# Loading and centring w_out ahead of chunk 1, and one table of 1/sqrt for chunk 0, in an attention-then-SoLU kernel

## The chip, the cores and the metric

The kernel runs on one core of one Trainium2 chip. The metric is the time of one execution in device microseconds (us). A profile is of one execution and its span is 1.7 to 1.8 us shorter than the timed run, so differences inside a profile are compared with differences inside another, and times with times.

## The reference, cut to what matters

```python
# q, k, v: (8, 8, 576, 64) float32
kv  = einsum('bhsd,bhse->bhde', k, v)                 # one 64x64 matrix per head
o   = einsum('bhsd,bhde->bhse', q, kv)
x   = o / sqrt(mean(o*o, -1) + 1e-6) * g_norm         # (4608, 512) after a transposition
h   = x @ w_in                                        # 512 -> 1024
solu = h * softmax(h)
out = layernorm(solu) * g_ln @ w_out                  # 1024 -> 512
```

The kernel folds the layer norm into the last product: `w_out` is scaled by `g_ln` and its column means are taken off ("centred") once, and each row of `out` is multiplied at the end by one number (`rstd`) that comes from three sums over `h` ("sums").

## The kernel before: what the change and the argument touch

The work is cut into nine chunks of 512 tokens. Every piece of work on an engine, and every load, is put into a plan with an engine, an estimated length and a rank. A small scheduler runs through the plan once, while the program is built, and the order that it finds is the fixed order of the instructions on each engine. On the chip only the engines' own order and the semaphores count: an engine that waits holds up everything behind it, and a transfer starts when its issuing engine comes to it.

```python
class Plan:
    def order(self):
        free, done, queue, lanes, mode = {}, {}, 0.0, [], {}
        ...
            done[n] = t + length + {"pe": 0.2, "sp": 2.5}.get(engine, 0.12)
            if load:                       # the model of a load: one queue, 'load' us each
                queue = max(queue, t + length + 1.0) + load
                done[n] = queue + 1.0
                lanes.append(done[n])
```

The loads are issued by POOL (GpSimd), which also does squares (`usq`) and sums of exponentials (`es`) between them. q of the chunks 0 to 3 is turned by TensorE; from chunk 4 on a transposing transfer, issued by SP, does it from SBUF to SBUF.

```python
    XBAR = tuple(range(4, NC))
    ...
    for b in range(B):
        behind = [] if b < 2 else [("x", (0, 1, 1))] if b == 2 else [("h_mm", b - 3, 2)]
        ...                                # k and v of chunk b: pool, load=3.0 each; q: pool, load=2.7
    plan.add("w_out", "pool", 0.9, -1.2, load_w_out, load=5.4)
    ...
    def q_turn(c):
        t = T["qT", c] = tile_of(("qT", c), [128, H, 2, 128], BF16)
        nc.sync.dma_start_transpose(
            t.rearrange("q h y p -> q (h y) p"), T["q", c].rearrange("p h j d -> p (h j d)")
        )
    ...
        if c in XBAR:
            plan.add(("qT", c), "sp", 4.0, r - 0.1, lambda c=c: q_turn(c), ...)
    ...
    def s_ln(*i):                          # 1/sqrt as exp(-0.5 ln): two passes on ACT
        nc.scalar.activation(out=t[:, :], in_=T["s", i][:, :], func=AF.Ln, bias=eps_t[:, :])
    def s_exp(*i):
        nc.scalar.activation(..., in_=T["lss", i][:, :], func=AF.Exp, scale=-0.5, bias=zero_t[:, :])
```

`h_mm` is h of a chunk (eight groups of four products), `out` the last product, `o_mm` the product of q with kv, and `usq` and `es` what POOL and ACT prepare for the sums.

The softmax here doesn't subtract the row's maximum and nothing guards it: scores larger than these inputs give would overflow.

## Time and profile before

| | before |
|---|---|
| time, median of 4 runs (range) | 202.06 us (200.93 to 203.91) |
| span of the profile, mean granted clock | 200.5 us, 1.00 |
| TensorE busy | 184.0 us, 92% of the span |
| third product of h (h goes on) | 22.29 us |
| sums of chunks 0, 1, 2, 3 begin | 47.01, 67.77, 85.89, 103.93 us |
| sums of the last chunk begin | 189.35 us |

The sums of each chunk are the landmarks of this document, because TensorE does them at the same place of its order in nearly all kernels below. They are read from the timeline of TensorE; the chain of waits, which the prediction used, has the same events 0.07 us later. Here is the table by stage, cut at these landmarks (columns: stretch, its length, busy time of TensorE, weight loads, DVE, ACT and POOL with counts of instructions, granted clock, DMA share, GB/s):

```profile
67.77:85.89 18.12, 18.12 (x162) 8.05 (x161) 12.59 (x23) 14.58 (x26) 15.03 (x16) 1.00 0.90 149
85.89:103.93 18.04, 18.04 (x162) 8.05 (x161) 12.76 (x24) 14.86 (x27) 14.58 (x16) 1.00 1.09 188
103.93:189.35 85.42, 85.42 (x735) 38.36 (x734) 57.11 (x103) 62.31 (x108) 55.76 (x53) 1.00 0.46 107
```

In each of the three TensorE's busy time is the whole stretch. A reader of this table alone would say that nothing but TensorE matters from 67 us on. What the table hides is how close the transfers behind it are. The timeline of POOL and that of SP around chunk 5 show it (start, length, engine and line, operation):

```profile
72.19 0.90 POOL L226 DMA_DIRECT2D q_sb<-in_q_dram  x1
...
85.76 1.94 SPq L311 DMA_TRANSPOSE qT_sb<-q_sb  x1
...
88.27 0.83 POOL L219 DMA_DIRECT2D k_sb<-in_k_dram  x1
```

q of chunk 5 is issued at 72.19 us, and SP can issue its transposition only when it has landed, at 85.76. The transposition takes 4.3 us. The next loads, those of chunk 6, are issued 2.5 us after it. TensorE comes to o of chunk 5 at 97.00 us and doesn't wait:

```profile
97.00 0.41 PE L326 MATMUL o_ps<-qT_sb,kvd 64*64 64x256 bf16 x8
```

So the transposition lands (85.76 + 4.3 = 90.1 us) 6.9 us ahead of its use. That is the slack which the table doesn't show.

### The profile page before, as it was taken

Reading aid. Unit: us, or ns where it says so; the run is one execution under the profiler, and the core shown is the slowest. Engines: PE = TensorE matmul, PEld = TensorE weight load, DVE = VectorE, ACT = ScalarE, POOL = GpSimd, SP = SyncE. Lnnn points to the kernel's source line nnn. Section 1 sums busy time; section 2 is a strip of 40 time slices with the busy share of each in tenths; the row PEclk is TensorE's granted clock in tenths of the full one; section 3 lists DMA queues with packets and bytes.
Section 4 is the critical chain, followed back from the end, with each engine's and each line's share of the span. In section 5 each row is a group of like instructions: output and inputs, shape, how many; then the busy total and the mean of one; then the engine's idle time right before and its main releaser. Section 6 shows DMA issues by size and latency. Waiting matters only on the chain.

```text
span 200.5 us, 4103 instructions
## 1 busy us (share of the span) xinstructions
PE 184.0 (92%) x1617; PEld 82.8 (41%) x1617; DVE 128.5 (64%) x244; ACT 135.6 (68%) x235; POOL 135.0 (67%) x143
## 2 busy tenths in 40 slices
PE   7887596689799999999999999999999999999990
PEld 2342252354254354435444443544445454444430
DVE  3343588559886668667586956876684757665350
ACT  2049589539478497969779696979679486556421
POOL 7973399999335987796697968386484828846200
PEclk9999999999999999999999999999999999999999
DMA  4999999999997269979999997836021111211206
GB/s 58 173 203 204 200 351 257 201 203 155 185 244 173 65 84 233 203 164 113 246 171 138 210 252 108 238 56 171 10 98 52 52 56 52 106 54 52 106 12 197
DMA packets 39986, 29.62 MB, mean 148 GB/s; under 512 B 11800, under 2 KB 34336, under 8 KB 39968
## 3 DMA queue, kind: packets, MB, share of 16 engines
q0 software_dynamic: 24208, 17.30, 57.0%
q1 hardware_dynamic: 15472, 11.54, 20.1%
q10 hardware_dynamic: 288, 0.52, 0.9%
q8 instruction: 12, 0.20, 0.4%
q14 instruction: 6, 0.05, 0.1%
HBM read 32.51 MB, written 9.44 MB: 209 GB/s over the span
## 4 chain that ended last, share of the span: by engine, by line
PE 73%; DMA 16%; DVE 3%; POOL 3%; issue 1%; ACT 1%; POOLq 0%
PE out_ps L550 29%; PE h_ps L429 26%; DMA v_sb<-in_v_dram 10%; DMA k_sb<-in_k_dram 6%; PE misc_ps L493 5%; PE s_ps L347 3%; PE o_ps L326 3%; PE misc_ps L281 3%; DVE w_out_sb L541 2%; PE o_ps L550 2%; PE misc_ps L301 1%; PE misc_ps L507 1%; POOL q_sb L226 1%; POOL w_in_sb L239 1%; DVE x_sb L362 1%
## 5 line engine op out<-in xcount | busy, mean ns | idle before, releaser
L429 PE MATMUL h_ps<-x_sb,w_in_sb 128*128 128x512 bf16 x288 | 74.2, 379 | 1.8 <-DVE x_sb L362 1.7
L550 PE MATMUL out_ps<-w_out_sb,u_sb 128*128 128x512 bf16 x272 | 69.7, 380 | 1.2 <-DVE w_out_sb L541 1.2
L461 POOL TENSOR_TENSOR es_sb<-e_sb 128x512 bf16<-128x512 f32 x36 | 45.8, 1272 | 31.8 <-ACT e_sb L437 31.7
L455 POOL TENSOR_TENSOR usq_sb<-u_sb 128x512 bf16<-128x512 bf16 x55 | 56.8, 1040 | 14.6 <-DVE u_sb L444 14.2
L437 ACT ACTIVATE e_sb<-h_ps,zero_t 128x512 f32<-128x512 f32 x72 | 49.2, 684 | 22.7 <-PE h_ps L429 22.2
L444 DVE TENSOR_TENSOR u_sb<-h_ps,e_sb 128x512 bf16<-128x512 f32 x72 | 49.3, 687 | 22.7 <-ACT e_sb L437 21.9
L429 PEld LDWEIGHTS <-w_in_sb 128*128 128x128 bf16 x288 | 26.9, 98 | 35.5 <-issue 6.0
L550 PEld LDWEIGHTS <-u_sb 128*128 128x128 bf16 x288 | 26.8, 98 | 34.4 <-issue 4.8
L560 DVE TENSOR_SCALAR ob_sb<-out_ps,rstd 128x512 f32<-128x512 f32 x33 | 24.6, 745 | 10.6 <-PE out_ps L550 6.2
L362 DVE SCALAR_TENSOR_TENSOR x_sb<-o_ps,g_rep,rst_sb 128x512 bf16<-128x512 f32 x32 | 23.9, 748 | 5.8 <-ACT rst_sb L355 5.8
L355 ACT ACTIVATE rst_sb<-lss_sb,zero_t 128x512 f32<-128x512 f32 x36 | 26.0, 723 | 0.6
L341 ACT ACTIVATE osq_sb<-o_ps,zero_t 128x512 bf16<-128x512 f32 x30 | 19.2, 682 | 10.4 <-PE o_ps L326 10.4
L351 ACT ACTIVATE lss_sb<-s_ps,eps_t 128x512 f32<-128x512 f32 x34 | 23.3, 686 | 1.0 <-PE s_ps L347 0.9
L453 ACT ACTIVATE usq_sb<-u_sb,zero_t 128x512 bf16<-128x512 bf16 x17 | 12.2, 720 | 3.9 <-DVE u_sb L444 3.9
L293 ACT CAST kvd<-misc_ps 64x256 bf16<-64x256 f32 (+1 forms) x20 | 6.5, 326 | 12.4 <-DVE kvd L291 10.2
L347 PE MATMUL s_ps<-osq_sb,head_mean 128*128 128x512 bf16 x34 | 13.0, 381 | 1.1 <-ACT osq_sb L341 1.0
L291 DVE CAST kvd<-misc_ps 64x256 bf16<-64x256 f32 (+1 forms) x20 | 7.2, 362 | 6.9 <-PE misc_ps L281 4.1
L194 PE MATMUL s_ps<-zeros 128*128 128x512 bf16 x28 | 9.8, 476 | 1.4 <-DVE zeros L155 1.2
L281 PE MATMUL misc_ps<-v_sb,k_sb 96*64 96x64 bf16 x384 | 8.0, 197 | 2.0 <-DMA v_sb<-in_v_dram 2.0
L226 POOL DMA_DIRECT2D q_sb<-in_q_dram x10 | 8.7, 872 | 1.5 <-POOLq L617 0.8
L219 POOL DMA_DIRECT2D k_sb<-in_k_dram x10 | 8.1, 807 | 2.3 <-DMA w_in_sb<-in_moe_w_in_dram 1.7
L281 PEld LDWEIGHTS <-k_sb 96*64 96x64 bf16 x384 | 7.0, 112 | 6.1 <-issue 6.1
(66 smaller groups left out, 126.5 us busy)
## 6 DMA issues: line engine op xcount, KB each, us to landing
out_dram<-ob_sb SPq DMA_DIRECT2D x34, 256.0 KB, 3.2
k_sb<-in_k_dram POOLq DMA_DIRECT2D x6, 576.0 KB, 8.1
v_sb<-in_v_dram POOLq DMA_DIRECT2D x6, 576.0 KB, 11.9
q_sb<-in_q_dram POOLq DMA_DIRECT2D x6, 512.0 KB, 14.8
w_out_f<-in_moe_w_out_dram POOLq DMA_DIRECT2D x1, 2048.0 KB, 17.2
k_sb<-in_k_dram POOLq DMA_DIRECT2D x4, 288.0 KB, 9.8
v_sb<-in_v_dram POOLq DMA_DIRECT2D x4, 288.0 KB, 10.4
q_sb<-in_q_dram POOLq DMA_DIRECT2D x4, 256.0 KB, 9.8
```

Source lines behind the costliest of these rows:

```text
L281: nc.tensor.matmul(t[hh * 64:hh * 64 + 64, n, :], T["k", b][:, h, i, :], T["v", b][:, h, i, :], start=(n == 0 and i == 0), stop=(i == 5), ...
L341: nc.scalar.activation(out=t[:, :], in_=T[("o", *i)].rearrange("p a b c -> p (a b c)"), func=AF.Square, bias=zero_t[:, :])
L351: nc.scalar.activation(out=t[:, :], in_=T["s", i][:, :], func=AF.Ln, bias=eps_t[:, :])
L355: nc.scalar.activation(out=t.rearrange("p a b c -> p (a b c)"), in_=T["lss", i][:, :], func=AF.Exp, scale=-0.5, bias=zero_t[:, :])
L362: nc.vector.scalar_tensor_tensor(out=T["x", c][:, 2 * hf:2 * hf + 2, z], in0=T["o", c, hf, z][:, :, :, :], scalar=g_rep[:, :], in1=T["rst" ...
L429: nc.tensor.matmul(t[:, :], w_in_sb[:, dt, f * 128:(f + 1) * 128], T["x", c][:, dt].rearrange("p a b c -> p (a b c)"), start=(dt == 0), st ...
L437: nc.scalar.activation(out=T["e", c, f // 2][:, f % 2, :], in_=T["h", c, f][:, :], func=AF.Exp, bias=zero_t[:, :])
L444: nc.vector.tensor_tensor(out=T["u", c][:, f, :], in0=T["h", c, f][:, :], in1=T["e", c, f // 2][:, f % 2, :], op=MUL)
L455: nc.gpsimd.tensor_tensor(out=dst, in0=src, in1=src, op=MUL)
L461: nc.gpsimd.tensor_tensor(out=T["es", c][:, n, :], in0=e[:, 0, :], in1=e[:, 1, :], op=ADD)
L550: nc.tensor.matmul(T["acc", c, m][:, :], T["u", c][:, f, m * 128:(m + 1) * 128], w_out_sb[:, f, :], start=(f == 0), stop=(f == NF - 1),)
L560: nc.vector.tensor_scalar_mul(out=t[:, :], in0=T["acc", c, m][:, :], scalar1=T["rstd", c][:, m:m + 1])
```

## The change

The intent: TensorE had 7.5 us of idle time between 20 and 54 us, part of it because w_out came late (the waits that end with its centring are 1.2 us). So w_out is loaded ahead of chunk 1, centred at once, and out of chunk 0 runs ahead of h of chunk 1; chunk 0's 1/sqrt takes one ACT pass from another table; and banks and engines of chunks 0 and 1 are dealt out again to suit. The scheduler's model of the loads gets two new constants.

```diff
-        free, done, queue, lanes, mode = {}, {}, 0.0, [], {}
+        free, done, queue, lanes, mode = {}, {}, 2.5, [], {}
-                done[n] = queue + 1.0
+                done[n] = queue + 1.3
-    nc.scalar.preload_act_table_set("natural_log_exp_and_others")
+    nc.scalar.preload_act_table_set("abs_reciprocal_sqrt_and_small")
+    plan.add("table", "act", 1.3, -1.0, lambda: nc.scalar.preload_act_table_set("natural_log_exp_and_others"),
+             [("ex", (0, hf, z)) for hf in range(2) for z in range(2)])
-        behind = [] if b < 2 else [("x", (0, 1, 1))] if b == 2 else [("h_mm", b - 3, 2)]
+        behind = [] if b < 2 else [("h_mm", 0, 0)] if b == 2 else [("h_mm", b - 3, 2)]
-    plan.add("w_out", "pool", 0.9, -1.2, load_w_out, load=5.4)
+    plan.add("w_out", "pool", 0.9, -1.55, load_w_out, load=5.4)
...  # chunk 0 and 1: kv copies and the copy of q of chunk 1 on ACT, other banks
+                if c == 0:
+                    plan.add(("ex", i), "act", 0.6, rz + 0.04, lambda i=i: s_rsqrt(*i), [("s_mm", i)], ...)
+        return ("h", "h", "o", "o", "out", "h", "h", "h")[f] if c == 0 else "h"
-            engine = "act" if f in ((2, 6) if c < NC - 1 else (1, 3, 5, 6, 7)) and c > 1 else "pool"
+            engine = "act" if f in {0: (2, 4, 6, 7), 1: (), NC - 1: (1, 3, 5, 6, 7)}.get(c, (2, 6)) else "pool"
...
+    plan.add("w_mean", "pe", 2.0, -0.5, lambda: [w_mean(f) for f in range(NF)], ["w_out", "g_mean", ("o_mm", 0, 1)],
+             first=[("out", "mean")])
-        r = c + 1
+        r, rs = (c + 1, c + 1) if c else (0.55, -0.5)
```

More of the change, by code (lines that the diff above doesn't have):

```diff
@@ L130, in tile_of @@
         return sb.tile(shape, dtype, name=key[0] + "_sb", tag=key[0], bufs=bufs[key[0]])
-    COPIED = ((0, 0), (1, 0), (1, 1))
+    COPIED = ((0, 0),)
     plan = Plan({**banks, **bufs})
     T = {}
-    nc.scalar.preload_act_table_set("natural_log_exp_and_others")
+    nc.scalar.preload_act_table_set("abs_reciprocal_sqrt_and_small")
     w_in_sb = big.tile([128, NP, d_ff], BF16, name="w_in_sb")
@@ L198 @@
         plan.add(("warm", "s", n), "pe", 0.45, 8.0, lambda: warm(2), ["warm"], first=[("s", "warm", n)])
-    for n, key in enumerate((("o_mm", 0, 0), ("s_mm", (0, 0, 0)), ("o_mm", 0, 1), ("s_mm", (0, 1, 0)))):
+    for n, key in enumerate((("o_mm", 0, 0), ("s_mm", (0, 0, 0)), ("o_mm", 0, 1))):
         plan.add(("warm", n), "pe", 0.65, 7.0, lambda: warm(3, "misc"), [key], first=[("misc", "warm", n)])
@@ L263 @@
                          first=[] if g else [(name, b)], load=3.0 / n)
-            plan.add(("q", b, g), "pool", 0.9 if n == 1 else 0.7, at + part + (-0.01 if b == 0 else 0.02 if b == 1 else 0.1),
+            plan.add(("q", b, g), "pool", 0.9 if n == 1 else 0.7, at + part + (0.02 if b < 2 else 0.1),
                      lambda b=b, hs=hs: load_q(b, hs), behind,
@@ L284, in kv_mm, with kv_engine @@
                     )
+    def kv_engine(b, hh):
+        return "act" if hh or b == 1 else "dve"
     def kv_copy(b, g, hs, hh, z):
@@ L289, in kv_copy @@
         src = T["kv", b, g][hh * 64:hh * 64 + 64, :, :]
-        if hh == 0:
+        if kv_engine(b, hh) == "dve":
             nc.vector.tensor_copy(dst, src)
@@ L305, in qT_copy @@
             T["qT", c] = tile_of(("qT", c), [128, H, 2, 128], BF16)
-        nc.vector.tensor_copy(T["qT", c][:, 4 * hf:4 * hf + 4], T["qTp", c, hf][:, :, :, :])
+        dst, src = T["qT", c][:, 4 * hf:4 * hf + 4], T["qTp", c, hf][:, :, :, :]
+        if c == 1:
+            nc.scalar.copy(dst, src)
+        else:
+            nc.vector.tensor_copy(dst, src)
     def q_turn(c):
@@ L357, in s_exp, with s_rsqrt @@
         )
+    def s_rsqrt(*i):
+        t = T["rst", i] = tile_of(("rst", i), [128, 2, 2, 128], FP32)
+        nc.scalar.activation(
+            out=t.rearrange("p a b c -> p (a b c)"), in_=T["s", i][:, :], func=AF.Abs_reciprocal_sqrt, bias=eps_t[:, :]
+        )
     def x_mul(c, hf, z):
@@ L378 @@
                     for z in range(2):
-                        plan.add(("kv", c, g, hh, z), "act" if hh else "dve", 0.34 if len(groups) == 1 else 0.25, rg + 0.05,
+                        plan.add(("kv", c, g, hh, z), kv_engine(c, hh), 0.34 if len(groups) == 1 else 0.25, rg + 0.05,
                                  lambda c=c, g=g, hs=hs, hh=hh, z=z: kv_copy(c, g, hs, hh, z), [("kv_mm", c, g)],
@@ L387 @@
             g = group(c, hf)
-            tag = "out" if c < 2 and hf else "o"
+            tag = ("out", "h")[c] if c < 2 and hf else "o"
             if c not in XBAR:
@@ L394 @@
                          ["ident", *loads], uses=[("q", c)] if c < B else [], first=[(qtag, "qT", c, hf)])
-                plan.add(("qT", c, hf), "dve", 0.62, (r + w * (0.12 + 0.1 * hf)) if c else -2.0, lambda c=c, hf=hf: qT_copy(c, hf),
+                plan.add(("qT", c, hf), "act" if c == 1 else "dve", 0.62 if c != 1 else 0.95, (r + w * (0.12 + 0.1 * hf)) if c else -2.0, lambda c=c, hf=hf: qT_copy(c, hf),
                          [("qT_mm", c, hf)] + ([("qT", c, 0)] if hf else []), uses=[(qtag, "qT", c, hf)] + ([("qT", c)] if hf else []),
@@ L415 @@
                          uses=[("osq", i)], first=[(stag, i)])
-                plan.add(("ln", i), "act", 0.6, rz + 0.03, lambda i=i: s_ln(*i), [("s_mm", i)],
-                         uses=[(stag, i)], first=[("lss", i)])
-                plan.add(("ex", i), "act", 0.6, rz + 0.04, lambda i=i: s_exp(*i), [("ln", i)],
-                         uses=[("lss", i)], first=[("rst", i)])
+                if c == 0:
+                    plan.add(("ex", i), "act", 0.6, rz + 0.04, lambda i=i: s_rsqrt(*i), [("s_mm", i)],
+                             uses=[(stag, i)], first=[("rst", i)])
+                else:
+                    plan.add(("ln", i), "act", 0.6, rz + 0.03, lambda i=i: s_ln(*i), [("s_mm", i), "table"],
+                             uses=[(stag, i)], first=[("lss", i)])
+                    plan.add(("ex", i), "act", 0.6, rz + 0.04, lambda i=i: s_exp(*i), [("ln", i)],
+                             uses=[("lss", i)], first=[("rst", i)])
                 plan.add(("x", i), "dve", 0.67, rz + 0.06, lambda i=i: x_mul(*i),
@@ L423, with h_bank @@
                          first=[("x", c)] if (hf, z) == (0, 0) else [])
+    def h_bank(c, f):
+        return ("h", "h", "o", "o", "out", "h", "h", "h")[f] if c == 0 else "h"
     def h_mm(c, f):
-        t = T["h", c, f] = bank(("h", c, f), [128, 512], FP32)
+        t = T["h", c, f] = bank((h_bank(c, f),), [128, 512], FP32)
         for dt in range(NP):
@@ L467 @@
             plan.add(("h_mm", c, f), "pe", 0.87, r, lambda c=c, f=f: h_mm(c, f),
-                     [("w_in", f // 4), *[("x", (c, *i)) for i in xs]], uses=[("x", c)], first=[("h", c, f)])
+                     [("w_in", f // 4), *[("x", (c, *i)) for i in xs]], uses=[("x", c)], first=[(h_bank(c, f), "h", c, f)])
             plan.add(("exp", c, f), "act", 0.57, r + 0.02, lambda c=c, f=f: h_exp(c, f),
-                     [("h_mm", c, f)] + ([("exp", c, f - 1)] if f % 2 else []), uses=[("h", c, f)] + ([("e", c, f // 2)] if f % 2 else []),
+                     [("h_mm", c, f), "table"] + ([("exp", c, f - 1)] if f % 2 else []), uses=[(h_bank(c, f), "h", c, f)] + ([("e", c, f // 2)] if f % 2 else []),
                      first=[] if f % 2 else [("e", c, f // 2)])
             plan.add(("u", c, f), "dve", 0.62, r + 0.04, lambda c=c, f=f: h_u(c, f),
-                     [("exp", c, f)] + ([("u", c, 0)] if f else []), uses=[("h", c, f), ("e", c, f // 2)] + ([("u", c)] if f else []),
+                     [("exp", c, f)] + ([("u", c, 0)] if f else []), uses=[(h_bank(c, f), "h", c, f), ("e", c, f // 2)] + ([("u", c)] if f else []),
                      first=[] if f else [("u", c)])
-            engine = "act" if f in ((2, 6) if c < NC - 1 else (1, 3, 5, 6, 7)) and c > 1 else "pool"
-            plan.add(("usq", c, f), engine, 0.57 if engine == "act" else 1.05, r + 0.15,
+            engine = "act" if f in {0: (2, 4, 6, 7), 1: (), NC - 1: (1, 3, 5, 6, 7)}.get(c, (2, 6)) else "pool"
+            plan.add(("usq", c, f), engine, 0.57 if engine == "act" else 1.05, r + 0.15 if c else -0.6,
                      lambda c=c, f=f, engine=engine: u_sq(c, f, engine), [("u", c, f)] + ([("usq", c, 0)] if f else []),
@@ L487, in sums @@
         if part == 0:
-            T["sum", c] = bank(("misc", "sum", c), [128, 512], FP32)
+            T["sum", c] = bank(("misc" if c else "h", "sum", c), [128, 512], FP32)
         i, src = ((1, T["u", c]), (0, T["usq", c]), (2, T["es", c]))[part]
@@ L569, in store @@
         (nc.scalar if c == NC - 1 and m % 2 else nc.sync).dma_start(dst[j], T["ob", c, m][:, :])
+    plan.add("w_mean", "pe", 2.0, -0.5, lambda: [w_mean(f) for f in range(NF)], ["w_out", "g_mean", ("o_mm", 0, 1)],
+             first=[("out", "mean")])
     for f in range(NF):
-        plan.add(("w_mean", f), "pe", 0.25, 0.2 + 0.05 * f, lambda f=f: w_mean(f),
-                 ["w_out", "g_mean", ("w_mean", f - 1) if f else ("o_mm", 1, 1)], uses=[] if f == 0 else [("out", "mean")],
-                 first=[("out", "mean")] if f == 0 else [])
@@ L575 @@
-        plan.add(("w_center", f), "dve", 0.67, 0.6 + 0.05 * f, lambda f=f: w_center(f), [("w_mean", NF - 1)],
-                 uses=[("out", "mean")])
+        plan.add(("w_center", f), "dve", 0.67, 0.05 + 0.12 * f, lambda f=f: w_center(f), ["w_mean"], uses=[("out", "mean")])
     for c in range(NC):
-        r = c + 1
+        r, rs = (c + 1, c + 1) if c else (0.55, -0.5)
         parts = [[("u", c, f) for f in range(NF)], [("usq", c, f) for f in range(NF)], [("es", c, n) for n in range(NF // 2)]]
-        plan.add(("sums", c), "pe", 1.2, r + 0.1, lambda c=c: [sums(c, part) for part in range(3)], sum(parts, []),
-                 uses=[("u", c), ("usq", c), ("es", c)], first=[("misc", "sum", c)])
@@ L582 @@
-        plan.add(("turn", c), "dve", 0.62, r + 0.14, lambda c=c: sums_turn(c), [("sums", c)],
-                 uses=[("misc", "sum", c)], first=[("sumT", c)])
-        plan.add(("st_mm", c), "pe", 0.15, r + 0.15, lambda c=c: stats_mm(c), ["fold", ("turn", c)],
+        plan.add(("sums", c), "pe", 1.2, rs + 0.1, lambda c=c: [sums(c, part) for part in range(3)], sum(parts, []),
+                 uses=[("u", c), ("usq", c), ("es", c)], first=[("misc" if c else "h", "sum", c)])
+        plan.add(("turn", c), "dve", 0.62, rs + 0.14, lambda c=c: sums_turn(c), [("sums", c)],
+                 uses=[("misc" if c else "h", "sum", c)], first=[("sumT", c)])
@@ L585 @@
+        plan.add(("st_mm", c), "pe", 0.15, rs + 0.15, lambda c=c: stats_mm(c), ["fold", ("turn", c)],
                  uses=[("sumT", c)], first=[("misc", "st", c)])
-        plan.add(("stats", c), "dve", 0.65, r + 0.16, lambda c=c: stats(c), [("st_mm", c)], uses=[("misc", "st", c)])
-        plan.add(("rstd", c), "act", 0.45, r + 0.17, lambda c=c: rstd(c), [("stats", c)])
+        plan.add(("stats", c), "dve", 0.65, rs + 0.16, lambda c=c: stats(c), [("st_mm", c)], uses=[("misc", "st", c)])
+        plan.add(("rstd", c), "act", 0.45, rs + 0.17, lambda c=c: rstd(c), [("stats", c)])
```

## The prediction

> **What bounds the kernel now.** The program works in nine chunks of 512 tokens. I read the page's slices first, for where its limits change.
>
> ```profile
> PE   7887596689799999999999999999999999999990
> DVE  3343588559886668667586956876684757665350
> DMA  4999999999997269979999997836021111211206
> ```
>
> One digit is 5 us. TensorE has no gap from the twelfth slice to the last but one; the DMA engines are full in the first sixty microseconds. So I cut the run at TensorE's landmarks and asked for the busy time in each stretch (columns: PE, PEld, DVE, ACT, POOL, clock, DMA share, GB/s).
>
> ```profile
> 19.98:54.00 34.02, 26.52 (x268) 12.36 (x267) 25.54 (x42) 22.60 (x40) 27.30 (x28) 1.00 1.30 222
> 54.00:67.84 13.84, 13.83 (x130) 6.79 (x132) 10.70 (x22) 11.13 (x20) 8.32 (x9) 1.00 0.93 188
> 85.96:189.40 103.44, 103.44 (x898) 46.38 (x902) 69.80 (x126) 77.10 (x134) 70.27 (x68) 1.00 0.57 121
> 189.40:200.50 11.10, 5.93 (x49) 2.35 (x48) 2.64 (x7) 1.97 (x4) 0.00 (x0) 0.99 0.31 94
> ```
>
> From 54 to 189 us TensorE is the bound, busy without a hole; the tail costs 5.2 us of idle. What can be won lies ahead of 54 us: the start of the first product with w_in ("h"), at 19.98 us, and 7.5 us of idle between there and 54 us. TensorE's order shows what stands there:
>
> ```profile
> 19.98 0.59 PE L429 MATMUL h_ps<-x_sb,w_in_sb 128*128 128x512 bf16 x2
> 22.29 0.59 PE L429 MATMUL h_ps<-x_sb,w_in_sb 128*128 128x512 bf16 x2 [1.71 <-DVE x_sb L362]
> 35.61 1.17 PE L535 MATMUL out_ps<-w_out_f,g_mean 128*128 128x512 f32 x4 [1.19 <-issue]
> 40.28 0.95 PE L281 MATMUL misc_ps<-v_sb,k_sb 96*64 96x64 bf16 x48 [1.24 <-DMA v_sb<-in_v_dram]
> 51.13 0.38 PE L550 MATMUL out_ps<-w_out_sb,u_sb 128*128 128x512 bf16 x1 [0.94 <-DVE w_out_sb L541]
> ```
>
> h of chunk 0 begins in earnest at 22.29 us, behind the last x. Then w_out is late: the column means of w_out (L535) run at 35.6 us, its centring (L541) at 45.1 to 51.7 us, so "out" of chunk 0 (L550) starts only at 48.6 us and TensorE lacks work meanwhile. The two ScalarE passes ahead of the last x, and the two transfers:
>
> ```profile
> 18.68 0.69 ACT L351 ACTIVATE lss_sb<-h_ps,eps_t 128x512 f32<-128x512 f32 x1
> 19.40 0.72 ACT L355 ACTIVATE rst_sb<-lss_sb,zero_t 128x512 f32<-128x512 f32 x1
> 20.03 0.67 ACT L351 ACTIVATE lss_sb<-s_ps,eps_t 128x512 f32<-128x512 f32 x1
> 20.73 0.72 ACT L355 ACTIVATE rst_sb<-lss_sb,zero_t 128x512 f32<-128x512 f32 x1
> ```
> ```profile
> 16.64 0.89 POOL L242 DMA_DIRECT2D w_out_f<-in_moe_w_out_dram  x1 [1.51 <-DMA w_in_sb<-in_moe_w_in_dram]
> 20.70 0.77 POOL L219 DMA_DIRECT2D v_sb<-in_v_dram  x1 [0.73 <-DMA k_sb<-in_k_dram]
> ```
>
> Issue plus time to landing gives: w_in 16.4 and 18.9; chunk 1's six half loads 20.4 to 27.4; w_out 16.6+17.2 = 33.8; chunk 2's k, v, q 37.3, 40.2, 42.9 us.
>
> **What the Trainium skill says.** "Perfetto Trace Analysis", Optimization Strategy: a kernel can have regimes, and one looks for gaps on the binding engine within a regime and interleaves regimes. The trace agrees: 7.5 us of gaps ahead of 54 us, none after. "ScalarE: Activation LUTs", What ACT_TABLE_LOAD costs: any function takes 280 + 0.833 N ns with a pointer bias, 707 ns for N = 512, and a switch of set 1.28 us plus 1.38 us of drain. The trace has 682 to 723 ns for the functions here and 1.28 us for the one load; nothing shows the drain. "DMA: Bandwidth & Descriptors", Queues, rings and completion order: each engine consumes a ring in order. The landings above come in order of issue, so moving w_out moves bytes and removes none. "TensorE: Matmul & The Clock Gate", What's actually happening: an idle window of about 3.4 us halves the clock. The longest idle here is 1.7 us and the granted clock is 1.00.
>
> **The change, part by part.** The order of instructions of both kernels shows that up to the sums of chunk 2 (85.96 us now), TensorE's real work is the same multiset, and from there on its order is identical. So the gain is how much earlier those sums start; being saturated, all later stages and the tail only shift.
>
> *Start of h.* k and v of chunk 0 now come ahead of q; the sum of bytes is the same, and the second half is complete at 13.8 us as now. q's transpose then becomes the last input: transpose to about 14.4, its DVE copy 14.45 to 15.15. Two groups of three warm-up products at 0.65 us hold "o" until 15.9; it ends at 16.3 (17.2 now). Then two squares (to 17.55, steps of 0.6), one 1/sqrt pass per tile in place of two, 17.6 to 18.85, two x multiplications at 0.67 to 0.75, and h goes on at 19.7. That is 2.6 us ahead of 22.29: 0.9 from "o" and 1.7 from the passes (two removed ones of 0.7 are 1.4).
> *Table load.* It starts at 18.9 and takes 1.3 us, while DVE makes x and TensorE the first h (done at about 20.2). Hidden; with the drain the first exp is 1.3 us late, but h has five banks now (h, h, o, o, out, at 0.87 us each), so TensorE does not notice.
> *w_out.* Behind w_in at 18.9 plus the 6.4 us it takes now (27.4 to 33.8): 25.3 us. Six h groups last until 24.5, then TensorE, in order, waits for it: 0.8 us idle. Means about 2.1 us, to 27.3; eight centrings at 0.67 us on DVE end at about 33, with u of f = 6 ahead of the last; u of f = 7 at 34.
> *Chunk 1* lands 27 to 33.9 us instead of 20.4 to 27.4, chunk 2 as before. From the waits in the order, its kv products, transposes and o go between h and out of chunk 0. TensorE's gaps that I find by hand: kv copies on ACT 0.5, ACT's longer copy of q (about 1.0 us for 1024 columns) 0.3 and 1.1 (the statistics product shares its bank), v of chunk 1 0.3, last centring and u 0.15, stats to rstd to the first output copy 1.0. With w_out's 0.8, about 4.2 us up to 47 us.
> *Chunk 1's h*, from 47 us: ACT has 20 passes at 0.6 us against some 12 us of TensorE's; o of chunk 2 waits for two x to free its banks (1.1), and two smaller ones: 1.8 us. POOL's squares (eight at 1.04, four sums at 1.27, three issues) end by 65.7 us, in time.
>
> *Sum.* TensorE's busy time from 19.98 to 67.84 (sums of chunk 1) is 40.35 us now. The new order has done 16 more h and out products by then (3.5 us), less 0.4 for h already done before 19.7 and some 0.9 for means in one piece and switches of tiling that fall into waits: 42.6. So those sums start at 19.7 + 42.6 + 5.4 = 67.7 (of the 6.0 us of gaps I take 5.4, since they overlap), against 67.84 + 3.5 = 71.3 for the same progress. Gain 3.6; were all mode switches hidden, 4.9. I take 4.1: span 196.4, and with the 1.8 us between span and timed run, **198.2 us**.
>
> **Rivals.** (a) *Transfers still set the pace.* Chunk 2's v is due at 40 and chunk 3's v at 48.7 whatever the order, as bytes up to there are equal; TensorE wants them at about 39.9 and 48.7. For it: DMA slices at 9 to 60 us. Against: no slack is needed beyond a microsecond. If w_out or chunk 1 land 1.5 us later, gain 2.5, 199.8 us. (b) *ACT becomes the bound between 28 and 60 us*: it gets four more kv copies, two q copies and four squares. For it: now 22.6 of 34 us busy there. Against: it loses four passes. If it stalls TensorE for 2 us more, 200.2. (c) *Everything fits*: author's order is calibrated, the gaps overlap, gain 5.5, 196.8. (d) *Slower*: a wrong order early costs over 4 us beyond my count; nothing points there.
>
> **Range and chances.** 198.2, from 196.2 (c, somewhat better) to 200.6 (a and b together in part). The 2% line is 198.25, on my number, so the first two verdicts are nearly even: faster 0.52, same 0.45, slower 0.03.
>
> **What would show it.** In the changed trace: the third product of h at 19.7 +- 0.8; w_out landing at 25.3 with a gap of 0.8 us ahead of the means; centrings 27 to 34; first out at 30 (48.6 now); a gap of about 1 us behind the transposes of chunk 1's second half; sums of chunk 2 at 81.9 (85.96 now), and the same distance from there to the end, 114.5 us. Wrong it would be if the distance after those sums changed, if h began after 21, or if gaps between 20 and 67 us came to more than 8 or less than 4 us.

## The result, and the profile after

| | before | after |
|---|---|---|
| time, median of 4 runs (range) | 202.06 us (200.93 to 203.91) | 211.57 us (210.89 to 212.37) |
| ratio, with 95% interval | | 1.0463 (1.0373 to 1.0552) |
| span of the profile, granted clock | 200.5 us, 1.00 | 210.6 us, 0.964 |

A ratio is the mean time of one kernel's fast runs over that of the other's of the same rounds, so it is not quite the ratio of the medians. Executions over 1.5% slower than the fastest of the same kernel are left out of the means. The changed kernel is **slower by 4.6%**, where about 2% faster was predicted.

The slices of the page (one digit is 5.3 us here) show where:

```profile
PE   7887798799799999991199999999999999999990
PEclk9999999979999999999559999999999999999998
```

TensorE has a hole of two slices at about 95 to 105 us, in the part that the prediction called saturated, and its clock is halved from about 100 us on. The clock has a second, smaller dent in the ninth slice. The table by stage, cut at the same landmarks, gives the sizes:

```profile
68.61:84.22 15.61, 15.19 (x145) 6.57 (x145) 11.28 (x21) 13.23 (x24) 13.94 (x16) 1.00 0.85 149
84.22:114.03 29.81, 20.83 (x162) 8.80 (x162) 13.37 (x24) 15.92 (x28) 15.44 (x16) 0.83 1.03 169
114.03:199.45 85.42, 85.42 (x735) 38.37 (x735) 56.97 (x103) 62.19 (x107) 55.56 (x52) 1.00 0.40 97
```

The sums of chunk 2 begin at 84.22, that is 1.67 us earlier than before: the start has gained. From the sums of chunk 3 to those of the last chunk it is 85.42 us, to the hundredth what it was. Between them the same 162 products take 29.81 us in place of 18.04: **11.77 us lost in one stretch**. And 11.77 - 1.67 = 10.1 us is the whole difference of the spans. The timeline of TensorE says what it waited for:

```profile
104.38 0.64 PE L333 MATMUL o_ps<-qT_sb,kvd 64*64 64x256 bf16 x8 [8.98 <-DMA qT_sb<-q_sb]
```

o of chunk 5 waited 8.98 us for the transposing transfer of q. The rest, 11.77 - 8.98 = 2.8 us, is clock. In stretches of 2 us (the third number from the right is the clock):

```profile
98.00:100.00 2.00, 0.00 (x0) 0.00 (x0) 0.00 (x0) 0.00 (x0) 0.00 (x0) 0.95 1.34 184
...
104.00:106.00 2.00, 1.62 (x11) 0.62 (x11) 0.00 (x0) 0.94 (x2) 0.00 (x0) 0.50 1.07 354
106.00:108.00 2.00, 2.00 (x6) 0.69 (x5) 0.00 (x0) 0.94 (x2) 0.00 (x0) 0.50 1.04 224
108.00:110.00 2.00, 2.00 (x6) 0.67 (x5) 0.69 (x1) 1.38 (x3) 0.65 (x1) 0.50 0.00 0
```

The clock is halved from 99.8 to 110 us. Of that, 104.4 to 110 us fall on work: 5.6 us at half speed cost 2.8.

Now the transfer. The timelines of POOL and SP, in the same places as those of before:

```profile
76.28 0.94 POOL L226 DMA_DIRECT2D q_sb<-in_q_dram  x1
...
87.24 0.82 POOL L219 DMA_DIRECT2D k_sb<-in_k_dram  x1
88.06 0.77 POOL L219 DMA_DIRECT2D v_sb<-in_v_dram  x1
88.82 0.91 POOL L226 DMA_DIRECT2D q_sb<-in_q_dram  x1
...
90.50 6.48 SPq L318 DMA_TRANSPOSE qT_sb<-q_sb  x1
```

The order has turned round: the three loads of chunk 6 are issued first, and the transposition of chunk 5 1.7 us after the last of them. It takes 13.8 us from issue to landing where it took 4.3, and SP's own instruction (the second number of its line) 6.48 us where it took 1.94. The queues of the DMA show the two together, in the microsecond from 99 to 100 us (queue: packets, MB, share):

```profile
q0 software_dynamic: 240, 0.12, 88.5%
q1 hardware_dynamic: 239, 0.06, 46.3%
```

q0 carries POOL's loads and q1 the transposition: 240 packets against 239. Before, in the microsecond from 87 to 88 us, q1 had the engines to itself and moved 830:

```profile
q1 hardware_dynamic: 830, 0.21, 109.8%
```

The page "DMA: Bandwidth & Descriptors" of the Trainium skill says in its section "Queues, rings and completion order" that each engine goes round between the queues it has work for, packet by packet. In this microsecond the counts of the trace agree; that what the trace counts as packets are the packets of the page isn't shown. The transposition's have 256 bytes and the loads' 512 here, so an even share of packets is a third of the bytes. The transposition also began late: between 90.6 and 94 us the trace has 801 packets of q0 and none of q1.

**First theory.** The change shifts chunk 5's loads against chunk 6's, so that the transposition of chunk 5 meets them; TensorE idles, and the idling halves the clock. **Rivals.** The transposition is late because q itself lands late, whatever is beside it; chunk 6's loads at that time hurt whatever comes; or the half clock comes first, from another cause, and the wait is only part of the story.

### The profile page after: what moved, and what is told of

Read it like the earlier page. It is cut to its first block, busy times and chain, and to the rows that moved or that the text cites. A ratio compares the mean times of both kernels' runs of the same rounds, so it can differ in the third digit from the quotient of the medians.

```text
span 210.6 us, 4090 instructions
## 1 busy us (share of the span) xinstructions
PE 186.7 (89%) x1614; PEld 84.0 (40%) x1614; DVE 125.4 (60%) x236; ACT 140.9 (67%) x244; POOL 128.8 (61%) x137
## 3 DMA queue, kind: packets, MB, share of 16 engines
q1 hardware_dynamic: 15472, 11.54, 19.4%
## 4 chain that ended last, share of the span: by engine, by line
PE 70%; DMA 15%; ACT 6%; POOL 3%; DVE 3%; issue 1%; POOLq 0%
PE out_ps L573 28%; PE h_ps L452 24%; DMA w_out_f<-in_moe_w_out_dram 8%; DMA qT_sb<-q_sb 7%; PE misc_ps L516 5%; PE o_ps L333 3%; PE s_ps L354 3%; ACT e_sb L460 2%; PE o_ps L573 2%; PE misc_ps L281 1%; PE out_ps L558 1%; ACT kvd L296 1%; ACT qT_sb L311 1%; ACT rst_sb L362 1%; PE misc_ps L304 1%
## 5 line engine op out<-in xcount | busy, mean ns | idle before, releaser
L452 PE MATMUL h_ps<-x_sb,w_in_sb 128*128 128x512 bf16 x276 | 71.3, 383 | 1.5 <-DVE x_sb L375 1.2
L573 PE MATMUL out_ps<-w_out_sb,u_sb 128*128 128x512 bf16 x272 | 71.6, 391 | 1.0 <-DVE ob_sb L583 0.7
L478 POOL TENSOR_TENSOR usq_sb<-u_sb 128x512 bf16<-128x512 bf16 x51 | 52.8, 1039 | 26.3 <-DVE u_sb L467 25.9
L467 DVE TENSOR_TENSOR u_sb<-h_ps,e_sb 128x512 bf16<-128x512 f32 x69 | 47.3, 688 | 35.2 <-ACT e_sb L460 34.5
L460 ACT ACTIVATE e_sb<-h_ps,zero_t 128x512 f32<-128x512 f32 x69 | 47.1, 684 | 16.8 <-PE h_ps L452 16.3
L362 ACT ACTIVATE rst_sb<-lss_sb,zero_t 128x512 f32<-128x512 f32 x32 | 23.2, 725 | 0.4
L476 ACT ACTIVATE usq_sb<-u_sb,zero_t 128x512 bf16<-128x512 bf16 x21 | 15.1, 721 | 4.2 <-DVE u_sb L467 4.1
L333 PE MATMUL o_ps<-qT_sb,kvd 64*64 64x32 bf16 (+1 forms) x240 | 8.8, 261 | 9.4 <-DMA qT_sb<-q_sb 9.0
L296 ACT CAST kvd<-misc_ps 64x128 bf16<-64x128 f32 (+1 forms) x24 | 7.5, 313 | 9.8 <-DVE kvd L294 9.1
L333 PEld LDWEIGHTS <-kvd 64*64 64x64 bf16 x256 | 4.7, 114 | 15.9 <-issue 13.5
```

What stands on the lines that cost most here:

```text
L333: nc.tensor.matmul(ts[z][hh * 64:hh * 64 + 64, pp, :, cols], kvd[rows, b, hh, 2 * hf + pp, :], T["qT", c][rows, 4 * hf + 2 * pp + hh, :, c ...
L362: nc.scalar.activation(out=t.rearrange("p a b c -> p (a b c)"), in_=T["lss", i][:, :], func=AF.Exp, scale=-0.5, bias=zero_t[:, :])
L452: nc.tensor.matmul(t[:, :], w_in_sb[:, dt, f * 128:(f + 1) * 128], T["x", c][:, dt].rearrange("p a b c -> p (a b c)"), start=(dt == 0), st ...
L460: nc.scalar.activation(out=T["e", c, f // 2][:, f % 2, :], in_=T["h", c, f][:, :], func=AF.Exp, bias=zero_t[:, :])
L467: nc.vector.tensor_tensor(out=T["u", c][:, f, :], in0=T["h", c, f][:, :], in1=T["e", c, f // 2][:, f % 2, :], op=MUL)
L478: nc.gpsimd.tensor_tensor(out=dst, in0=src, in1=src, op=MUL)
```

## The experiments

Most edits change the order of POOL's instructions alone: the scheduler's list is taken as it is, and named pieces are put ahead of another piece before the program is built. Where an edit does more, its text says so. All kernels gave correct results. There were thirteen runs on four chips, one of them of the unedited changed kernel and one a repeat of an edit; "before" ran in the same rounds each time, and each ratio is to that.

### Chunk 6's and 7's loads later

```diff
-    for fn in plan.order():
-        fn()
+    todo = plan.order()            # now a list of (name, function)
+    # k, v, q of chunk 6 to just ahead of ("usq", 3, 3); k, v, q of chunk 7 ahead of ("usq", 4, 3)
+    for _, fn in todo:
+        fn()
```

> The changed kernel with one edit: on GpSimd the three loads of chunk 6 and of chunk 7 are issued a few instructions later, so that the transposing transfer of the q of chunk 5 (issued at 90.5 us) no longer stands beside 3.4 MB of loads. TensorE's, VectorE's, ScalarE's and SyncE's orders are unchanged. Theory 1 (the transposing transfer shares the DMA engines packet by packet with loads issued just ahead of it): it lands in 4.3 to 5 us in place of 13.8, TensorE's 9.0 us wait shrinks below 1 us, the half clock after it is gone, the span falls by 10 to 12 us to about 199 to 200.5 (time 200 to 202). Theory 2 (the transposing transfer is late because the q of chunk 5 itself lands late at 90.5, or is slow for another reason such as the stores): issue and landing stay about as they are, and the span stays above 206.

Measured: 199.09 us (198.83 to 199.22, four runs), ratio 0.9843 (0.9798 to 0.9889). From the timelines of SP and POOL of this run:

```profile
89.16 1.85 SPq L318 DMA_TRANSPOSE qT_sb<-q_sb  x1
...
90.59 0.82 POOL L219 DMA_DIRECT2D k_sb<-in_k_dram  x1
```

The transposition is issued 1.4 us ahead of the first load and takes 4.3 us. The stretch between the sums of chunks 2 and 3 is 18.04 us again, and the mean granted clock of the run is 0.998. The sums of chunk 2 begin at 82.85 us. Nothing was done to q of chunk 5, which lands as long after those sums as in the changed kernel (6.3 us), so q's landing alone isn't the cause. But it decides how much of a slow transposition shows. In the changed kernel o of chunk 5 was due at 104.38 - 8.98 = 95.40 us, and even a transposition of 4.3 us would have landed at 94.8: of the 6.9 us of slack before the change, 0.6 were left.

### Only v and q of chunk 6, and chunk 7, later

```diff
-    # k, v, q of chunk 6 to just ahead of ("usq", 3, 3)
+    # v, q of chunk 6 to just ahead of ("usq", 3, 3); k stays where the change has it
```

> A dose between the changed kernel and the one with the loads issued late: of chunk 6 only k (a third of the bytes) is issued where the changed kernel issues it, v and q late. Theory 1: the landing of the transposing transfer of chunk 5 lies between 5 and 9 us, about 7, and TensorE waits 0 to 4 us for it; time about 200 to 205. Theory 2: 13 us as in the changed kernel.

Measured: the transposition took 10.5 us, a value between 4.3 and 13.8, TensorE waited 3.1 us for it, and the half clock came at about 98 to 101 us. The one fast run took 203.7 us; the other three, 207.36 to 209.19 us, were slow, so the times tell little. The transfer took longer than the 5 to 9 us expected, but this isn't the effect of k alone. v and q of chunk 6 were issued at 90.26 and 91.04 us, behind the transposition (86.27) but before it was done. By microseconds, the trace has the first packets of the transposition's queue at about 90.8 us; by 94.0 us 2048 of them, that is all of its data, had gone. From 94.0 to 95.75 us only packets of the loads follow, then 30 small ones of its queue, and it counts as landed at 96.8. So k alone held up the start by about as much as three loads do, and the end came only behind packets of v and q. The run is no clean dose.

### The mirror: chunk 6's loads earlier in the kernel before

```diff
 # the kernel before
+    # k, v, q of chunk 6 to just ahead of ("q_last", 2)
```

> The mirror: the kernel before with the three loads of chunk 6 issued some 5 us earlier on GpSimd, at about 83.5 us, ahead of the transposing transfer of chunk 5 at 85.8. Theory 1: that transfer takes 10 to 14 us in place of 4.3 and lands at 96 to 100; o of chunk 5 is due at 97.1 us, so TensorE waits 0 to 3 us for it, perhaps with a spell of half clock; time 202 to 207. Theory 2: it still takes 4.3 us, and the time stays at 202.

Measured: 205.04 us (203.9 to 206.06), ratio 1.0138 (1.0075 to 1.02). With the loads ahead of it, the same transposition of the kernel before takes 13.9 us in place of 4.3. TensorE waits 1.6 us for it; the transposition was issued 0.1 us ahead of the sums of chunk 2, at 84.84 us, and not 6.3 us behind them as in the changed kernel, so most of it was hidden. The mechanism needs nothing of the change; the size of the loss does.

### TensorE kept busy just before the sums' small products

```diff
 # on top of the later loads
+    # five products of zeros on TensorE just ahead of ("st_mm", 0)
```

> The kernel with the loads issued late, and five more warm-up products on TensorE in the 1.1 us in which it waits at 38.9 us for ScalarE's copy of q of chunk 1. Theory on the clock: the granted clock of 0.5 between 41.9 and 45.9 us comes from TensorE doing little in the 3 to 4 us ahead (idle, transposes, products with 12 or 64 columns), so filling the gap keeps it at 1.00, and the span falls by 1.5 to 2.2 us against the kernel with the loads late (to about 197.5 to 198.5). Rival: the dip has another cause (power, a fixed phase after the start), and stays: span within 0.5 us of the other.

Inconclusive. Two of four runs were slow. The profiled one was, too: w_out landed at 28.2 us in place of 25.9, TensorE waited 2.9 us for it, and the half clock came right there (28 to 32 us). The dent at 42 us that this run was to remove was gone in the run without the filler as well. It isn't tied to the order of instructions, and it comes in some runs only.

### q of chunks 5, 6 and 7 loaded ahead of k and v

```diff
+    # q of chunk 5 to just ahead of k of chunk 5; the same for 6 and 7
```

> The changed kernel with one edit: for chunks 5, 6 and 7 POOL issues the load of q ahead of those of k and v instead of behind them; chunk 6's loads stay as early as the change has them. If the 9.0 us wait comes from the transposing transfer of chunk 5 meeting chunk 6's loads in the queues, q now lands some 4 to 8 us sooner (82 to 86 us in place of 90.5), the transposition is issued before chunk 6's loads (87 us) or at most with them, it takes 4.3 to 6 us, TensorE's wait for it goes, and the time is 198.5 to 200.5 us. If the earliness of chunk 6's loads itself were what costs (rival: more load traffic beside the stores and kv copies at that time), the time stays at 205 us or more, with the transposition quick or not.

Measured: 201.92 us (201.03 to 203.26), ratio 0.9915 (0.9839 to 0.9991). This is my miss: the transposition was issued at 81.61 us, 4.3 us ahead of chunk 6's first load, and still took 15.9 us, since it now ran beside k and v of its own chunk. It landed in time, but it slowed those loads in turn: the last of the three, v, took 17.0 us from issue to landing, where the last of the three takes 14.2 us with the later loads, and TensorE waited for it:

```profile
91.05 1.28 PE L281 MATMUL misc_ps<-v_sb,k_sb 96*64 96x64 bf16 x48 [2.52 <-DMA v_sb<-in_v_dram]
```

So it isn't chunk 6 alone that matters: the transposition's first 4 us, in which nearly all of it would have gone without loads, fell before chunk 6's first load. Later chunk 6's loads were in the queue too, and there the even round isn't what the trace shows: from 88 to 92 us q1 moved 1021 packets and q0 229, so the transposition had most of the packets and still only a third of its rate alone (830 in a microsecond). For that I have no reading.

### Two parts undone, one part alone

```diff
 # on top of the later loads: chunk 0's 1/sqrt by Ln and Exp again, one table
 # on top of the later loads: w_out's rank back
-    plan.add("w_out", "pool", 0.9, -1.55, load_w_out, load=5.4)
+    plan.add("w_out", "pool", 0.9, -1.2, load_w_out, load=5.4)
 # the kernel before: chunk 0's 1/sqrt by one pass, second table behind it, nothing else
```

In these three the scheduler orders all engines anew.

> The kernel with the loads of chunks 6 and 7 late (199.1 us) and, of the change, only the rsqrt part undone: chunk 0 takes its 1/sqrt by Ln and Exp again, one table from the start. If the prediction's sizes hold, h goes on about 1.4 us later (21.3 in place of 19.9 us), and since TensorE then waits less for w_out (1.2 us of wait) part of it comes back: sums of chunk 1 0.3 to 1.4 us later, time 199.4 to 200.6 us. If the rsqrt part is worth nothing because w_out's landing sets the pace anyway, under 0.3 us. If it is the larger part of the gain at the start, 2 us or more.

> The kernel with the loads of chunks 6 and 7 late (199.1 us) and, of the change, only the early load of w_out undone: w_out goes behind the loads of chunk 1 again, so lands at about 33.8 us in place of 25.9; the planner then moves the centrings behind and out of chunk 0 with them. If the early w_out carries the gain, TensorE's idle time between 20 and 67 us grows by 2 to 4 us and the time goes to 201 to 203 us. If the order of the rest (the other banks and engines) carries it, the time stays within 0.7 us of 199.1.

> The kernel before with the rsqrt part alone: chunk 0's four 1/sqrt by one pass each, the second table loaded after them. If removed passes are worth what the prediction says, h goes on 1.4 us earlier (20.9 in place of 22.29 us), of which w_out, which still lands at 33.8 us, takes back a part: sums of chunk 1 0 to 1.4 us earlier than 67.84 and the time 201.0 to 202.4 us. The loads of chunk 6 and the transposition of chunk 5 shift together, so if the late theory holds the transposition keeps its 4.3 us as long as it is still issued first; if chunk 6's loads come first here, it takes 10 to 14 us and the time is 203 us or more, whatever the start gained.

| | time (range) | ratio | sums of chunk 2 | half clock in the profile |
|---|---|---|---|---|
| Ln and Exp again | 203.19 (202.41 to 203.4) | 0.9985 (0.9924 to 1.0045) | 85.97 | 23.0 to 26.4 us |
| w_out behind chunk 1 again | 204.53 (203.98 to 205.89) | 1.0067 (0.9999 to 1.0136) | 86.76 | 33.2 to 46.8 us |
| rsqrt alone on before | 203.75 (202.88 to 204.31) | 1.0016 (0.9951 to 1.008) | 87.78 | 3.4 us twice |

Each kernel with a part undone has lost about all of the gain, and the rsqrt part alone gains nothing although h goes on at 19.84 us in place of 22.29. But the sizes that I expected aren't what is measured here. Where Ln and Exp are back, TensorE waits 2.40 us for the last x and then works at half clock for some 3.4 us, which costs up to 1.7 of the 3.1 us; the remaining 1.4 is what two passes should cost, but since the whole order is new, that isn't shown. With w_out late, TensorE waits 1.78 and 1.25 us close together, and the clock stays at 0.5:

```profile
34.00:46.00 12.00, 10.29 (x90) 5.39 (x90) 7.37 (x12) 7.25 (x12) 1.28 (x1) 0.50 1.34 201
```

All four runs of this kernel have the same mean clock of 0.962. Waits and clock can't be separated in these three, so the single terms of the sum stay unsized.

### q of chunk 5 turned by TensorE

```diff
-    XBAR = tuple(range(4, NC))
+    XBAR = (4, 6, 7, 8)
```

> The changed kernel, its loads where the change has them (chunk 6's early), but q of chunk 5 is turned by TensorE and DVE, as q of chunks 0 to 3 is, and not by a transposing transfer. If the meeting of that one transfer with chunk 6's loads is the cause, the 9.0 us wait and the half clock after it go, TensorE gets 1.2 us of transposes more, and the time is 199.5 to 202 us, with q of chunk 5 landing at 90 us as in the changed kernel. If q's late landing is the cause (rival), the transposes wait for q and the time stays above 205 us. If the loads of chunk 6 slow whatever comes then, some other transfer, such as the transposition of chunk 6, takes over 8 us and TensorE waits for that.

Measured: 201.05 us (200.13 to 201.5), ratio 0.9919 (0.9872 to 0.9965); the unedited changed kernel on the same chip took 210.22. Chunk 6's loads are as early as the change has them (85.68 us), but there is no transposition for them to meet. q lands at 89.1 us, 6.4 us after the sums of chunk 2, as in the changed kernel. TensorE doesn't wait for q of chunk 5, there is no half clock in the profile, and the other transpositions take 4.3 to 4.9 us. The stretch between the sums of chunks 2 and 3 is 19.11 us, 1.1 more than 18.04, against the 1.2 expected for the transposes. That clears q's landing and the early loads as causes of their own.

### The wait filled with work that does nothing

```diff
+    # 40 products of zeros into an unread bank on TensorE, just ahead of ("o_mm", 5, 0)
```

> The changed kernel with 40 products of zeros (8.6 us at full clock, written to a bank nobody reads) put on TensorE just ahead of the o of chunk 5, that is into the 9.0 us wait. They remove no wait. If the half clock from 99.8 to 110 us comes from TensorE's idling, the granted clock there stays at 1.00 and the time is 2 to 3.5 us under the changed kernel of the same chip (about 208 to 209.5 us). If the half clock has another cause (power, or the transfers), it stays 0.5 after the wait, the products themselves take up to 17 us, and the time is 211 to 216 us.

Measured: 208.49 us (207.29 to 209.37) against 210.22 on the same chip. The transposition still took 14.9 us, but TensorE did not idle:

```profile
93.27 8.80 PE L194 MATMUL s_ps<-zeros 128*128 128x512 bf16 x39
102.00 0.41 PE L333 MATMUL o_ps<-qT_sb,kvd 64*64 64x256 bf16 x8
```

The granted clock is 1.00 all through, and the stretch between the sums of chunks 2 and 3 takes 26.67 us in place of the 29.44 of the unedited kernel on this chip (its run is the next one), 2.8 us less. Not all of that is clock: the transposition was issued sooner here (4.1 us after the sums of chunk 2, against 6.4), so o of chunk 5 began 0.6 us sooner after those sums. From the start of o to the sums of chunk 3 it is 6.92 us in place of 9.12: 2.2 us, about what half clock cost in that unedited run (29.44 - 18.04 - 9.13 of wait = 2.3). Over the four runs the difference of the medians is 1.7 us, a little under the 2 to 3.5 expected. So the half clock here is a consequence of the idling and no cause of its own.

### The changed kernel again, and the later loads again

> The changed kernel itself, unedited, on this chip, as the one to compare the other runs of this call with. Expected 209 to 212.5 us with the wait of 8 to 10 us for the transposition of chunk 5 and a stretch of half clock after it; the half clock at 42 to 46 us in some runs only (mean granted clock 0.964 with it and 0.972 without, if that reading of the earlier four runs is right), worth about 1.2 us.

Measured: 210.22 us (208.5 to 211.51), ratio 1.0372 (1.0313 to 1.0432). The wait is 9.13 us and the transposition takes 13.9 us. The dent of the clock at 42 us is absent, and the sums of chunk 2 begin at 82.43 us, 3.5 us earlier than before.

> The kernel with the loads of chunks 6 and 7 late again, unchanged, in five rounds on another chip, to see whether it beats the kernel before by over 2% or by less. Expected ratio 0.980 to 0.989, time 198.5 to 200 us, mean granted clock 0.99 or more, all transpositions 4.3 to 4.6 us. If the 0.984 of the first time was the chip's or the day's, the ratio is 0.99 or above.

Measured: 200.41 us (198.79 to 204.29, six runs, one of them slow), ratio 0.9895 (0.9845 to 0.9944). All transpositions of the profiled run took 4.3 to 4.7 us. The ratio is just outside the expected 0.980 to 0.989. The gain over before is real on both chips: 1.6 and 1.0% by the means, 0.6 to 2.0% by the intervals. One fast run had 201.43 us at a clock of 0.997, for which I have no reading.

### Chunk 5's loads back at their old distance

What was still open was why the two meet. Relative to the sums of chunk 2, chunk 6's k is issued 3.0 us after them in the changed kernel (87.24 - 84.22) and 2.4 us before the change (88.27 - 85.89), so it has about kept its place. q of chunk 5 is issued 7.9 us ahead of them (84.22 - 76.28) where it was 13.7 (85.89 - 72.19). POOL's timeline in the changed kernel has the reason. These are the first line of a stretch in which it has no hole, and the line that follows the next hole; the bracket gives the idle time ahead of the instruction:

```profile
51.65 1.04 POOL L478 TENSOR_TENSOR usq_sb<-u_sb 128x512 bf16<-128x512 bf16 x1 [16.40 <-DVE u_sb L467]
...
80.78 1.27 POOL L484 TENSOR_TENSOR es_sb<-e_sb 128x512 bf16<-128x512 f32 x1 [1.25 <-ACT e_sb L460]
```

With out of chunk 0 done first, h of chunk 1 comes late and all at once. POOL idles for 16.4 us and then works off its squares and sums for 28 us without a hole, with the loads of chunks 4 and 5 between them.

```diff
+    # k, v, q of chunk 5 to just ahead of ("es", 2, 0); chunk 6 stays where the change has it
```

> The changed kernel with chunk 6's loads where the change has them, and k, v and q of chunk 5 moved together some 5 to 6 us earlier on POOL (to about 67 to 69 us, which is where they stood in the kernel before, counted from the sums of chunk 2: 15.3 and 13.7 us ahead of them). If the meeting comes from chunk 5's loads being issued late against TensorE's progress, q of chunk 5 now lands at 81 to 84 us, its transposition has moved most of its bytes before chunk 6's loads are issued at 85 to 87 us, takes 4.3 to 6 us, TensorE doesn't wait for it, and the time is 198.8 to 200.8 us. The transposition of chunk 4 (65 to 70 us) now meets chunk 5's loads instead and may take 8 to 12 us, hidden if TensorE wants it at about 77 us. If the transposition of chunk 5 still takes over 10 us, or the time stays over 205 us, the lateness of chunk 5's loads isn't what brings the two together.

Measured: **198.90 us** (198.46 to 198.97), ratio 0.9823 (0.9744 to 0.9901).

```profile
68.69 0.90 POOL L226 DMA_DIRECT2D q_sb<-in_q_dram  x1
...
83.42 1.86 SPq L318 DMA_TRANSPOSE qT_sb<-q_sb  x1
...
85.70 0.83 POOL L219 DMA_DIRECT2D k_sb<-in_k_dram  x1
```

The transposition is issued 2.3 us ahead of chunk 6's loads, takes 4.3 us, and TensorE doesn't wait for it. The stretch between the sums of chunks 2 and 3 is 18.04 us. The transposition of chunk 4 meets the loads of chunk 5 now and takes 6.5 us (8 to 12 expected), hidden. This version and the later loads are the fastest; q first and q of chunk 5 by TensorE are ahead of both kernels too, by 0.8% with intervals below 1. None is shown to be over 2% faster than before: the intervals of this run and of the first run of the later loads contain 0.98, the others lie above it.

| profiled run | sums of chunk 2 | from there to sums of chunk 3 | transposition of chunk 5 | span |
|---|---|---|---|---|
| before | 85.89 | 18.04 | 4.3 | 200.5 |
| after | 84.22 | 29.81 | 13.8 | 210.6 |
| after, again | 82.43 | 29.44 | 13.9 | 208.4 |
| wait filled | 82.25 | 26.67 | 14.9 | 205.4 |
| k of chunk 6 early | 82.50 | 22.91 | 10.5 | 201.9 |
| q first | 82.86 | 22.20 | 15.9 | 201.5 |
| q of 5 by TensorE | 82.67 | 19.11 | none | 198.4 |
| later loads | 82.85 | 18.04 | 4.3 | 197.4 |
| chunk 5 earlier | 82.68 | 18.04 | 4.3 | 197.2 |
| before, chunk 6 early | 84.97 | 20.76 | 13.9 | 202.1 |

## Why the prediction was wrong, point by point

*The step that failed* is the one that carried the early gain to the end: "being saturated, all later stages and the tail only shift", with "the same distance from there to the end, 114.5 us". The distance became 210.6 - 84.3 = 126.3 us (84.3 is the same event in the chain's time). The prediction named this as what would make it wrong, and then did not test it against anything but the order on TensorE. That order was indeed identical. What changed was the order *between* two queues that nothing ties to each other: POOL's loads and SP's transposition, which before were 2.5 us apart. A busy TensorE showed only that its inputs came in time, not by how much (6.9 us here, of which the shift used up 6.3). With chunk 5's loads put back at their old distance, and nothing else touched, the distance from those sums to the end is 197.2 - 82.7 = 114.5 us, and the time is 198.9 against the predicted 198.2.

*Rival (a), transfers still set the pace,* looked at landings of loads only, and was put aside with "no slack is needed beyond a microsecond". The transposition is a transfer too, and was in none of the four rivals. The statement about POOL, that its squares would end "by 65.7 us, in time", was made for the sums; what stands behind those squares in POOL's order, chunk 5's loads, was not followed.

*The clock.* "The longest idle here is 1.7 us and the granted clock is 1.00" was true and was taken as safe. It was also a lucky profile: of the 31 fast runs of the kernel before that ran beside the experiments, 19 have a mean clock under 0.99, down to 0.976. After the 9 us wait the half clock cost 2.8 us more (2.3 in the repeat), and with the wait filled it was gone. The half clock's lengths, worked out from the stretches of 2 us, are 3.4 us (q first, k early, Ln and Exp), 10.2 us (the changed kernel, both profiles) and 13.6 us (w_out late): once, three and four times 3.4. "TensorE: Matmul & The Clock Gate" of the Trainium skill, "What's actually happening", has a free-running window of about that length, and the traces agree with the length. An idle stretch of a whole window wasn't needed: single waits of 1.77, 2.40 and 2.52 us were followed by it (rsqrt alone, Ln and Exp again, q first).

*Start of h.* Predicted 19.7, measured 19.93, and 19.4 in the repeat. Right.

*Table load.* In the changed kernel's trace ACT loads the second table at 19.03 to 20.31 us and the first exponential follows at 20.56, as soon as its h is there. Hidden, as predicted.

*w_out.* Predicted to land at 25.3 with 0.8 us of wait; measured 25.9 and 1.2. Means at 26.05 us, centrings from 28.2 to 34.1 (27 to 34 predicted), the first out at 31.18 (30 predicted). Right, half a microsecond to one late.

*The gap behind chunk 1's second transposes,* "about 1 us": measured 1.1 us, for ACT's copy of q.

*Sum.* The sums of chunk 2 were to come 4.1 us earlier. In the changed kernel's first profile it is 1.7; in the repeat 3.5, and in the seven other profiles with the same early order on the other engines 3.0 to 3.6. So the term was oversized by 0.5 to 1.1 us (the idle time of TensorE between 20 and 67 us, 5.1 us in the changed kernel, was within the 4 to 8 predicted), and in the first profile a half clock of some 3.4 us at 42 to 45 us, which is not in all runs, took the rest.

*What stays open.* The single worths of the rsqrt and of the early w_out, since undoing either brings waits that cost clock as well. Also why the transposition's first packet comes 4 to 4.5 us after its issue when loads are ahead of it (1.1 us in the kernel before), and why SP's instruction then takes 6.0 to 6.5 us in place of 1.9: the runs show that it meets loads, not by what means they hold it up.

## What to carry to other kernels

An engine that is busy without a hole tells nothing of the slack of what feeds it: before a shift is called harmless, list the transfers of each later stage with issue, landing and first use, and look for pairs on different queues whose order rests on a margin of a few microseconds. An issuing engine that also computes moves its loads when its work is moved, so follow what stands *behind* the moved work in its order. And count a TensorE wait of some 2 us or more at more than its length, since half clock may follow it.

## What the Trainium skill lacked or had wrong

- "Advanced Engine Details and Errata", X-Bar Transpose (TRN2), has transposing DMAs "as fast as regular DMAs" and expects 350 to 400 GB/s. Here one of 128 x 2048 bf16 elements (0.52 MB) took 4.3 us, and in a microsecond in which its queue had the engines alone 830 packets of 256 bytes went through, 212 GB/s.
- No page says what a transposition costs beside loads of another queue: 10.5 us with one load of chunk 6 ahead and two behind, 13.8 to 14.9 with three ahead, 15.9 beside its own chunk's k and v and then chunk 6's loads. The round of the queues by packets on "DMA: Bandwidth & Descriptors" would let one foresee the even share (240 against 239), but neither the first packet's delay of about 4 us nor the 1021 against 229 packets in the last of these cases.
- "TensorE: Matmul & The Clock Gate" puts the half clock, in the table of "What's actually happening", after an idle window of about 3.4 us. Single waits of 1.77, 2.40 and 2.52 us were followed by half clock, and waits of 1.78 and 1.25 us close together by 13.6 us of it, while single waits of 1.71 (before) and 1.43 us (later loads) were not, in their profiled runs.
